# A cached-attention decode step: one load for the last two V tiles, and dummy matmuls on both sides of them

## The chip, the cores and the metric

The kernel runs on one core of a Trainium2 chip. The metric is the device time of one execution in microseconds (us). The kernel before takes 381.98 us, the median of three runs (381.79 to 382.12).

In what follows PE is the matmul engine (TensorE), DVE the vector engine, ACT the scalar engine, SP the engine whose queue issues the large loads. L464 is line 464 of the kernel.

## What is computed

One token (a row x of 1024) goes through two branches whose results are mixed by a gate. Branch A is attention with a cache of 65,536 positions: 32 query heads share 4 heads of K and V, each head 128 wide. Branch B is a small gated MLP.

```python
g = sigmoid((x * gate_w).sum(-1))
q = (x @ wq)                                   # 32 heads of 128
scores = einsum('bhqd,bhkd->bhqk', q, k) * 128 ** -0.5
p = softmax(scores)                            # over 65,536 positions
a = einsum('bhqk,bhkd->bhqd', p, v).reshape(1, 1, 4096) @ wo
b = branch_B(x)
out = g * a + (1 - g) * b                      # 1 x 1 x 1024, bf16
```

K and V are 4 x 65,536 x 128 in bf16 each, 67 MB each. With the weights some 162 MB are read for one row of output.

## The kernel before

One SBUF buffer `kv` has five places of 32 KB per partition. A K or V head is cut into four tiles (j = 0 to 3), each as large as one place, 4.2 MB. A load may span two places. All loads go through the one queue of SP, in program order; a load is issued when the last readers of its places are done.

```python
kv = big.tile([P, NKV * CT * P], BF16, name="kv")      # P = CT = 128, NKV = 5

def load_kv(src, g, j, at, n=1):                       # n tiles from tile j, into place `at`
    h, i = divmod(j, 2)
    rows = src[0, g, 2 * h * CT * P:2 * (h + 1) * CT * P, :].rearrange(
        "(p c) d -> p (c d)", c=2 * CT)
    v = load(rows[:, i * CT * DH:(i + n) * CT * DH], (n * CT * DH,), at)
    return [v[:, i * CT * DH:(i + 1) * CT * DH] for i in range(n)]
```

For every tile of V, 64 columns of probabilities are loaded as weights 16 times and two matmuls of 512 columns follow each load: 32 matmuls (L464). They go alternately to the upper and the lower half of the output's partitions and add up in one PSUM tile over all four tiles of the head.

```python
def v_tile(g, j, vt):
    ...
    for u in range(CC // 2):                           # CC = 32
        hs = slice(u % 2 * P // 2, (u % 2 + 1) * P // 2)
        for e in range(2):
            ins = nc.tensor.matmul(o_ps[g][hs, e, :], lhsT=ptt[g, j][:, 2 * u:2 * u + 2, :]...,
                                   rhs=vx[:, 2 * u + e], ...)          # L464
            if e > 0:
                same_weights(ins)                      # the second weight load is dropped
```

After the fourth tile `head_out` reduces this PSUM tile on DVE, sums over groups with two pairs of small matmuls on PE, divides by the softmax's sum and writes 32 rows of `oa`.

```python
def head_out(g):
    nc.vector.tensor_tensor(out=om8, in0=o_ps[g]..., in1=own_8..., op=ALU.mult)   # L474
    nc.vector.tensor_reduce(out=o_sb[:], in_=om8..., op=ALU.add)                  # L478
    nc.tensor.matmul(om_ps[gs, DH:], lhsT=hs, rhs=lss[g][:], ...)                 # L482
    nc.tensor.matmul(om_ps[gs, :DH], lhsT=hs, rhs=o_sb[:], ...)                   # L484
    ...                                                                           # five small DVE operations
    nc.vector.tensor_scalar(out=oa[gs, :], in0=osum[gs, :], ...)                  # L496

def keep_busy(n):                                      # dummy matmuls, their result is never read
    ps = pss.tile([P, 2 * HN], FP32, name="busy_ps", tag="s")
    for i in range(n):
        nc.tensor.matmul(ps[:, :HN], lhsT=w[:, :P], rhs=w[:, :HN], ...)           # L503, 128x128x512
```

The end of the kernel is the last head's V, its output, and then the projection with `wo`, which comes in five loads. Dummy matmuls stand where PE would have nothing to do. PE executes in program order.

```python
for j, n, at in ((0, 2, 2), (2, 1, 1), (3, 1, 0)):     # tiles 0 and 1, then 2, then 3
    for i, vt in enumerate(load_kv(A_v_cache, G - 1, j, at, n)):
        v_tile(G - 1, j + i, vt)
keep_busy(6)
head_out(G - 1)
keep_busy(16)

for n in (24, 4, 2, 1, 1):                             # of 32 pieces of wo, 256 KB each
    t = load(wo_view[:, c0:c0 + n, :], (n, D), 3 + c0 * D / (CT * P))   # places 3 and 4
    project(t, n, oa, c0, last=(c0 + n == OC))         # 4 n matmuls of 256 columns, L514
    keep_busy(WO_BUSY[n])                              # 24: 0, 4: 2, 2: 1, 1: 0
    c0 += n
nc.scalar.copy(out=out_sb[:], in_=out_ps[:])           # L566, then the store
```

Of the kernel before, what the change touches and what calls it, by code (L numbers as in the profile page):

```python
# [29 lines left out]
def kernel(  # L30
# [18 lines left out]
    _, G, S, DH = A_k_cache.shape  # L49
# [30 lines left out]
    def same_weights(ins):  # L80
        held.add(ins.ins.name)
# [95 lines left out]
    def load(src, shape, at):  # L177
        n = 1
        for s in shape:
            n *= s  # L180
        v = kv[:, int(at * CT * P):int(at * CT * P) + n]
        if len(shape) == 2:
            v = v.rearrange("p (a b) -> p a b", b=shape[1])
        ins = nc.sync.dma_start(out=v, in_=src)  # L184
        if not first_load:
            first_load.append(ins.ins.name)
        return v

    def load_kv(src, g, j, at, n=1):
# [5 lines that stand above are left out]
# [166 lines left out]
    for k in range(NHB):  # L361
# [3 lines left out]
                                                                   j=B, e=2),  # L365
# [91 lines left out]
    def v_tile(g, j, vt):  # L457
        if j == 0:
            o_ps[g] = pso.tile([P, 2, VC * DH], FP32, name="o_ps")
        vx = vt.rearrange("p (v c d) -> p c v d", v=VC, d=DH)  # L460
        for u in range(CC // 2):
            hs = slice(u % 2 * P // 2, (u % 2 + 1) * P // 2)
            for e in range(2):
                ins = nc.tensor.matmul(  # L464
                    o_ps[g][hs, e, :],
                    lhsT=ptt[g, j][:, 2 * u:2 * u + 2, :].rearrange("p c x -> p (c x)"),
                    rhs=vx[:, 2 * u + e], start=(j == 0 and u < 2),
                    stop=(j == NT - 1 and u >= CC // 2 - 2), skip_group_check=True)
                if e > 0:
                    same_weights(ins)  # L470

    def head_out(g):
        gs = slice(g * B, (g + 1) * B)
        nc.vector.tensor_tensor(  # L474
            out=om8, in0=o_ps[g][:].rearrange("p e (v d) -> p (e v) d", d=DH),
            in1=own_8[:].unsqueeze(2).to_broadcast([P, 2 * VC, DH]), op=ALU.mult)
        o_sb = wk.tile([P, DH], FP32, name="o_sb")
        nc.vector.tensor_reduce(out=o_sb[:], in_=om8.rearrange("p x d -> p d x"), axis=AX.X,  # L478
                                op=ALU.add)
        om_ps = psm.tile([P, DH + NT], FP32, name="om_ps", tag="m")  # L480
        hs = hsel[:].rearrange("p h q -> p (h q)")
        nc.tensor.matmul(om_ps[gs, DH:], lhsT=hs, rhs=lss[g][:], start=True, stop=True,  # L482
                         skip_group_check=True)
        nc.tensor.matmul(om_ps[gs, :DH], lhsT=hs, rhs=o_sb[:], start=True, stop=True,  # L484
                         skip_group_check=True)
        rl = wk.tile([P, 2], FP32, name="rl")
        nc.vector.reduce_sum(out=rl[gs, 0:1], in_=om_ps[gs, DH:], axis=AX.X)
        nc.vector.reciprocal(out=rl[gs, 1:2], in_=rl[gs, 0:1])
        om = wk.tile([P, QD, OC], FP32, name="om")
        nc.vector.tensor_tensor(  # L490
            out=om[gs], in0=om_ps[gs, :DH].rearrange("p (q c) -> p q c", c=OC),
            in1=own_q[gs, :].unsqueeze(2).to_broadcast([B, QD, OC]), op=ALU.mult)
        osum = wk.tile([P, OC], FP32, name="osum")
        nc.vector.tensor_reduce(out=osum[gs, :], in_=om[gs].rearrange("p q c -> p c q"),
                                axis=AX.X, op=ALU.add)
        nc.vector.tensor_scalar(out=oa[gs, :], in0=osum[gs, :], scalar1=rl[gs, 1:2],  # L496
                                scalar2=gate[gs, :], op0=ALU.mult, op1=ALU.mult)

    def keep_busy(n):
        ps = pss.tile([P, 2 * HN], FP32, name="busy_ps", tag="s")  # L500
        w = wt[G % 2][:].rearrange("p v b t u h -> p (v b t u h)")
        for i in range(n):
            ins = nc.tensor.matmul(ps[:, :HN], lhsT=w[:, :P], rhs=w[:, :HN], start=True,  # L503
                                   stop=True, skip_group_check=True)
            if i > 0:
                same_weights(ins)
# [22 lines left out]
    for g in range(1, G):  # L529
# [16 lines left out]
            if h == 0 and g + 1 < G:  # L546
                build_w(g + 1)
        head_out(g - 1)
    for j, n, at in ((0, 2, 2), (2, 1, 1), (3, 1, 0)):
        for i, vt in enumerate(load_kv(A_v_cache, G - 1, j, at, n)):  # L550
            v_tile(G - 1, j + i, vt)
    keep_busy(6)
    head_out(G - 1)
    keep_busy(16)

# [54 lines left out]
```

## Time and profile before

| | |
|---|---|
| time, median of three | 381.98 us |
| span of the profiled execution | 380.5 us |
| read from memory | 162.01 MB, 426 GB/s over the span |
| PE busy | 226.4 us, 60% |
| DVE busy | 211.2 us, 56% |
| ACT busy | 39.6 us, 10% |
| mean granted clock of PE | 0.839 of full speed |

The profile is that of one execution. A busy share is an average over the whole span. The row of slices cuts the span in 40 equal parts of 9.5 us; a digit is the busy share in tenths. The chain that ended last is followed back from the last instruction, at each step to what released it. The timeline lists the instructions of an engine in order of time, runs of the same kind merged; in brackets stands how long the engine was idle before and what ended that. A table by windows gives, for each stretch, its length, the busy time of PE, of its weight loads, of DVE, ACT and GpSimd (with the number of instructions), then the clock granted to PE (1.00 is full speed), the busy share of the DMA engines, and GB/s.

Matmuls are pipelined, so the time of a group is the distance from its first start to its last end, and the lengths of single matmuls in it overlap.

### The profile page before, as it was taken

The page shows a single profiled execution, that of the slowest core. Times are in us where ns is not written, and L with a number is a line of the kernel's source. Part 1 is how long each engine was busy: PE and PEld are TensorE (multiplying, and loading weights), DVE is VectorE, ACT ScalarE, POOL GpSimd, SP SyncE. Part 2 cuts the span into 40 slices and gives each one's busy share as a digit, 9 for nine tenths or more (in the row PEclk, how much of TensorE's full clock was granted, in tenths as well). Part 3 has the DMA queues.
Part 4 walks back from the last instruction along what each step waited for, and adds up shares of the span by engine and source line. Part 5 has one row for each costly group of instructions (what it writes and reads, how often), then busy time and mean ns, then how long its engine had stood idle before and what let it go on. Part 6 is the DMA issues. An engine that isn't in the chain of part 4 may idle for free.

```text
span 380.5 us, 2602 instructions
## 1 busy us (share of the span) xinstructions
PE 226.4 (60%) x1397; PEld 55.6 (15%) x800; DVE 211.2 (56%) x207; ACT 39.6 (10%) x55; POOL 4.4 (1%) x10
## 2 busy tenths in 40 slices
PE   0060605967655784794499139762993197739386
PEld 0010101211211210121022001110220011202113
DVE  4134217989374947867893058678940397650040
ACT  1001000111104310114011001140110010500000
POOL 4000000000000000000000000000000000000000
PEclk9995765999958796999599758995898599959789
DMA  9999999999999999999999999999999999999995
GB/s 386 476 420 413 401 442 441 441 472 410 407 422 441 441 443 434 434 434 441 441 429 441 434 441 420 422 413 442 434 434 429 427 434 442 436 410 434 431 432 224
DMA packets 3655, 162.17 MB, mean 426 GB/s; under 512 B 440, under 2 KB 444, under 8 KB 828
## 3 DMA queue, kind: packets, MB, share of 16 engines
q1 hardware_dynamic: 3604, 162.01, 98.8%
q8 instruction: 8, 0.13, 0.1%
q14 instruction: 3, 0.02, 0.0%
q10 hardware_dynamic: 40, 0.01, 0.0%
HBM read 162.01 MB, written 0.00 MB: 426 GB/s over the span
## 4 chain that ended last, share of the span: by engine, by line
DMA 71%; PE 17%; DVE 9%; issue 2%; SPq 0%; ACTq 0%; ACT 0%; DVEq 0%
DMA kv<-in_A_k_cache_dram 52%; PE s_ps L419 13%; DVE kv L412 8%; DMA kv<-in_A_wo_dram 7%; DMA kv<-in_A_v_cache_dram 7%; DMA wb<-in_B_b_sp_dram 5%; PE o_ps L464 2%; PE z_ps L296 1%; SPq L184 0%; DVE mx L402 0%; ACTq L198 0%; PE small_ps L271 0%; ACT out_sb L566 0%; PE out_ps L514 0%; ACTq L199 0%
## 5 line engine op out<-in xcount | busy, mean ns | idle before, releaser
L419 PE MATMUL s_ps<-kv,wt 128*128 128x512 bf16 x512 | 132.8, 414 | 81.4 <-DVE kv L412 81.3
L412 DVE STREAM_TRANSPOSE kv<-kv 128x2048 int32<-128x2048 int32 x64 | 142.4, 2280 | 69.7 <-DMA kv<-in_A_k_cache_dram 69.7
L464 PE MATMUL o_ps<-kv,pt 128*64 128x512 bf16 x512 | 63.6, 408 | 14.3 <-DMA kv<-in_A_v_cache_dram 14.3
L419 PEld LDWEIGHTS <-wt 128*128 128x128 bf16 x256 | 26.4, 103 | 189.2 <-issue 117.9
L428 ACT CAST sc<-s_ps 128x1024 bf16<-128x1024 f32 x16 | 16.2, 1013 | 250.7 <-PE s_ps L419 250.7
L464 PEld LDWEIGHTS <-pt 128*64 128x64 bf16 x256 | 16.9, 117 | 57.9 <-issue 48.6
L454 DVE STREAM_TRANSPOSE pt<-sc 128x1024 bf16<-128x1024 bf16 x16 | 18.6, 1217 | 6.8 <-ACT sc L451 6.8
L474 DVE TENSOR_TENSOR rowt<-o_ps,own 128x1024 f32<-128x1024 f32 x4 | 4.8, 1195 | 26.5 <-PE o_ps L464 26.5
L451 ACT ACTIVATE sc<-sc,nb 128x1024 bf16<-128x1024 bf16 x16 | 18.2, 1137 | 12.2 <-DVE nb L447 12.2
L484 PE MATMUL om_ps<-o_sb,hsel 128*32 128x128 f32 x8 | 2.3, 388 | 18.3 <-DVE o_sb L478 18.3
L402 DVE TENSOR_TENSOR mx<-mx,sc 128x1024 bf16<-128x1024 bf16 x8 | 5.5, 687 | 13.6 <-ACT sc L428 13.6
L296 PE MATMUL q_ps<-kv,xT 128*32 128x512 bf16 x64 | 5.7, 534 | 7.2 <-DMA kv<-in_A_wq_dram 7.2
L252 PE MATMUL xb_ps<-xg,spread 8*128 8x256 bf16 x1 | 0.4, 364 | 13.5 <-DMA xg<-in_gate_w_dram 13.5
L478 DVE TENSOR_REDUCE o_sb<-rowt 128x128 f32<-128x1024 f32 x4 | 7.5, 1872 | 0.1
L363 DVE TENSOR_TENSOR rowt<-q_ps,own_b 128x512 f32<-128x512 f32 x2 | 1.3, 686 | 10.8 <-PE q_ps L296 10.8
L503 PE MATMUL busy_ps<-wt 128*128 128x512 bf16 x25 | 6.1, 381 | 0.0
L296 PE MATMUL z_ps<-kv,xT 128*32 128x448 bf16 x64 | 6.1, 572 | 0.0
L566 ACT CAST out_sb<-out_ps 128x256 bf16<-128x256 f32 x1 | 0.4, 372 | 46.4 <-PE out_ps L514 46.4
L256 DVE TENSOR_TENSOR xm<-xb_ps,sel_i 128x128 f32<-128x128 f32 x2 | 0.5, 286 | 8.2 <-PE xb_ps L252 8.2
L514 PE MATMUL out_ps<-kv,oa 128*32 128x256 bf16 x128 | 4.2, 273 | 1.4 <-DMA kv<-in_A_wo_dram 1.4
L435 DVE TENSOR_REDUCE m<-mx 128x1 f32<-128x1024 bf16 x4 | 4.8, 1209 | 0.1
L296 PEld LDWEIGHTS <-xT 128*32 128x32 bf16 x64 | 2.6, 137 | 14.7 <-issue 14.6
(90 smaller groups left out, 61.2 us busy)
## 6 DMA issues: line engine op xcount, KB each, us to landing
kv<-in_A_v_cache_dram SPq DMA_DIRECT2D x2, 4096.0 KB, 22.8
kv<-in_B_w_in_dram SPq DMA_DIRECT2D x1, 7168.0 KB, 19.7
kv<-in_A_wo_dram SPq DMA_DIRECT2D x1, 6144.0 KB
kv<-in_B_w_out_dram SPq DMA_DIRECT2D x1, 3584.0 KB
kv<-in_A_wo_dram SPq DMA_DIRECT2D x1, 1024.0 KB, 26.8
kv<-in_A_wo_dram SPq DMA_DIRECT2D x1, 512.0 KB
kv<-in_A_wo_dram SPq DMA_DIRECT2D x2, 256.0 KB
kv<-in_A_k_cache_dram SPq DMA_DIRECT2D x8, 27.6
```

The costliest lines, as they stand in the source:

```text
L296: ins = nc.tensor.matmul(ps[t * B:(t + 1) * B, k * HN:k * HN + n], lhsT=xT[:, i * KH + c:i * KH + c + 1].to_broadcast([P, B]), rhs=w[:, c, ...
L402: nc.vector.tensor_tensor(out=mx[:], in0=mxs[g][:], in1=sc[:], op=ALU.max)
L412: nc.vector.transpose(out=kb[:, v * n:(v + 1) * n], in_=kb[:, v * n:(v + 1) * n])
L419: ins = nc.tensor.matmul(s_ps[:, k * HN:(k + 1) * HN], lhsT=wt[g % 2][:, v, b].rearrange("p a v h -> p (a v h)"), rhs=kx[:, b // 2, b % 2, ...
L428: nc.scalar.copy(out=sct[g, j][:], in_=s_ps[:])
L435: nc.vector.reduce_max(out=m1[:], in_=mxs[g][:], axis=AX.X)
L451: nc.scalar.activation(out=sct[g, j][:], in_=sct[g, j][:], func=ACT.Exp, scale=SCALE, bias=nb[:, 0:1], accum_out=lss[g][:, j:j + 1])
L454: nc.vector.transpose(out=ptt[g, j][:].rearrange("p c x -> p (c x)"), in_=sct[g, j][:])
L464: ins = nc.tensor.matmul(o_ps[g][hs, e, :], lhsT=ptt[g, j][:, 2 * u:2 * u + 2, :].rearrange("p c x -> p (c x)"), rhs=vx[:, 2 * u + e], sta ...
L474: nc.vector.tensor_tensor(out=om8, in0=o_ps[g][:].rearrange("p e (v d) -> p (e v) d", d=DH), in1=own_8[:].unsqueeze(2).to_broadcast([P, 2 ...
L478: nc.vector.tensor_reduce(out=o_sb[:], in_=om8.rearrange("p x d -> p d x"), axis=AX.X, op=ALU.add)
L503: ins = nc.tensor.matmul(ps[:, :HN], lhsT=w[:, :P], rhs=w[:, :HN], start=True, stop=True, skip_group_check=True)
```

## The change

Tiles 2 and 3 of the last head's V come in one load of 8.4 MB into places 0 and 1, where there were two loads of 4.2 MB. After tiles 0 and 1, PE gets 24 dummy matmuls; after tiles 2 and 3 it gets 6, as before. The 16 behind the head's output stay. The dummies are there to keep PE from idling while it waits for a load[...]. Nothing of the result changes.

```diff
-    for j, n, at in ((0, 2, 2), (2, 1, 1), (3, 1, 0)):
-        for i, vt in enumerate(load_kv(A_v_cache, G - 1, j, at, n)):
+    for j, at in ((0, 2), (2, 0)):
+        for i, vt in enumerate(load_kv(A_v_cache, G - 1, j, at, 2)):
             v_tile(G - 1, j + i, vt)
-    keep_busy(6)
+        keep_busy((24, 6)[j // 2])
     head_out(G - 1)
     keep_busy(16)
```

In the order of instructions PE gains the 24 dummies (and their one weight load) between tile 1 and tile 2, and tile 3 no longer has a wait for a load of its own. SP has one load less. The other engines' instructions are the same.

## The prediction

> **What bounds the kernel now.** I read the row of slices first. All 40 slices of the DMA row read 9 but the last, at 426 GB/s over the span, while PE is busy 60% and DVE 56%. So the stream of loads is the bound as a whole, and a change that moves no bytes can only act where the stream ends. Next the chain that ended last, by line, and the end of the same chain in order of time:
>
> ```profile
> DMA 71%; PE 17%; DVE 9%; issue 2%; SPq 0%; ACTq 0%; ACT 0%; DVEq 0%
> ...
> 350.46 27.89 DMA kv<-in_A_wo_dram
> 378.39 0.32 PE out_ps L514 x4
> 378.73 0.37 ACT out_sb L566
> ```
>
> The columns of the last three are start, length, what. The end hangs on the last piece of wo, landed near 378.35; behind it stand only four matmuls, one copy and the store. Then the timeline of PE over the last stage (start, length, engine, line, operation; in brackets the idle time before it and what ended it):
>
> ```profile
> 339.43 9.20 PE L464 MATMUL o_ps<-kv,pt 128*64 128x512 bf16 x64 [2.11 <-DMA kv<-in_A_v_cache_dram]
> 349.14 3.65 PE L464 MATMUL o_ps<-kv,pt 128*64 128x512 bf16 x32 [0.52 <-DMA kv<-in_A_v_cache_dram]
> 358.86 6.26 PE L464 MATMUL o_ps<-kv,pt 128*64 128x512 bf16 x32 [6.08 <-DMA kv<-in_A_v_cache_dram]
> 365.05 1.47 PE L503 MATMUL busy_ps<-wt 128*128 128x512 bf16 x6
> 366.45 0.23 PE L482 MATMUL om_ps<-ls,hsel 128*32 128x4 f32 x2
> 368.34 0.41 PE L484 MATMUL om_ps<-o_sb,hsel 128*32 128x128 f32 x2 [1.67 <-DVE o_sb L478]
> 368.68 3.63 PE L503 MATMUL busy_ps<-wt 128*128 128x512 bf16 x16
> 373.41 3.24 PE L514 MATMUL out_ps<-kv,oa 128*32 128x256 bf16 x112 [1.10 <-DMA kv<-in_A_wo_dram]
> ...
> 378.39 0.29 PE L514 MATMUL out_ps<-kv,oa 128*32 128x256 bf16 x4 [0.28 <-DMA kv<-in_A_wo_dram]
> ```
>
> To be seen: tile 2 of V is used up (349.14 to 352.79) while tile 3 is on its way; tile 3 lands at about 358.85. Before the projection PE waits 1.10 us for wo, before its last four matmuls 0.28 us. These 1.38 us are all the room that PE has behind tile 3.
>
> Last the granted clock (PEclk, third figure from the end; 1.00 full, 0.50 half) in windows cut where it changes:
>
> ```profile
> 118.44:121.85 3.41, 1.15 (x7) 0.37 (x3) 0.65 (x3) 2.28 (x2) 0.00 (x0) 1.00 1.20 519
> 350.54:353.96 3.42, 2.24 (x22) 0.68 (x9) 0.00 (x0) 0.00 (x0) 0.00 (x0) 1.00 0.91 393
> 353.96:357.37 3.41, 0.00 (x0) 0.00 (x0) 0.00 (x0) 0.00 (x0) 0.00 (x0) 1.00 1.07 461
> 357.37:360.78 3.41, 1.92 (x10) 0.58 (x5) 0.00 (x0) 0.00 (x0) 0.00 (x0) 0.50 1.07 461
> 360.78:364.20 3.42, 3.42 (x18) 0.91 (x8) 0.00 (x0) 0.00 (x0) 0.00 (x0) 0.50 1.03 446
> ```
>
> The first figure behind the length is PE's busy time. Stepping the whole trace in this way puts every change of the clock on one grid of 3.41 us. At full clock a window with 0.34 or less of PE busy (1.15 of 3.41 at 118.44) was followed by half clock, one with 0.42 or more (1.43 at 77.48) was not. At half clock 0.81 or more (2.77 at 125.27) brought it back, 0.72 or less (2.44 at 108.20) did not. I take the middles, 0.38 and 0.77.
>
> [...] two joined V or K loads land between 300.67 and 339.38, 19.36 us each; tiles 2 and 3 as two loads take from 339.38 to 358.82, 19.44 us.
>
> **The change part by part.**
>
> The load. One 8.4 MB load for two of 4.2 MB. Both were issued at 331.01, some 8 us ahead of their turn, and wo at 348.66, 10 us ahead of its own, on the matmuls of tile 1, which stand before the new dummies. The queue runs dry in neither form. Gain at the landing: 19.44 - 19.36 = 0.08 us, which I count as none. Tile 3 still lands near 358.85, but tile 2 now counts as landed only then too.
>
> The matmuls that move. The 32 matmuls of tile 2, 3.65 us hidden under tile 3's transfer before, now stand behind 358.85 with the other 32.
>
> The 24 dummies. At full clock 16 take 3.63 us (0.227 each), so 24 take 5.45 us: about 348.65 to 354.1. They leave PE idle for 358.85 - 354.1 = 4.75 us. Two neighbouring windows cannot share 4.75 us without one of them having 2.37 idle, busy share 0.30 or less. So the clock falls wherever the grid lies: the dummies are too few by about 1 us to hold it. What the grid decides is when it comes back.
>
> Time T of the 64 matmuls. Elsewhere in this trace 64 of the kind take 7.10 us at full clock (the group at 203.70). At half clock four take 0.85 us against 0.43, so a cold stretch c adds 0.495 c. (Check: tile 3, cold until 364.20, c = 5.34: 3.65 + 2.64 = 6.29, measured 6.26.) Let p be the time from the landing to the next edge of the grid. [...] I take p anywhere in 0 to 3.41:
> - p under 0.8: the clock is still up at the landing, falls at the edge, returns a window later; c = 3.41, T = 8.8.
> - p from 0.8 to 2.65: cold at the landing, that window too little busy; c = p + 3.41, T = 9.2 to 10.1, 9.6 on average.
> - p over 2.65: cold, back at the edge; c = p, T = 8.4 to 8.8.
>
> Weighted by 0.80, 1.85 and 0.76 of 3.41 the mean is 9.2 us.
>
> From there to the end. Before, tile 3 ends at 365.12 and the 16 dummies at 368.68 + 3.63 = 372.31, 7.19 us later. The projection with its dummies takes 4.99 us from its start if wo is there (373.41 to 378.68, less 0.28). So PE ends at 358.85 + T + 7.19 + 4.99 = 371.03 + T against 378.68: **the loss is T - 7.65**, nothing where that is negative. With 9.2 it is 1.55 us, from 0.8 to 2.5. In this the 16 dummies are the later wait: oa is ready 4.97 us after tile 3 (365.12 to 370.09), 373.0 with T = 9.2, the dummies end at 375.2. The first 6.3 MB of wo land at 373.41, the next 1.05 MB at 430 GB/s by 375.9, before PE has worked through the first.
>
> **Rivals.**
>
> *The clock holds.* If the bridge is good enough, T = 7.1, below 7.65: PE is ready before wo, nothing changes, 381.9. The aim of the change speaks for it; the 4.75 us gap against the 0.34 windows speaks against it. It would take dummies that run longer than 0.227 each or an earlier landing.
>
> *The load is hidden or a little faster.* The tail is DMA-bound, so a lower cost of the single load is the only thing that can shorten it: 0.08 us, 381.9. A saving several times that would need the boundary between two loads to cost time, and the DMA row shows no dip at 349. I give this little.
>
> *The dummies as the bound.* The 24 could delay tile 2 if they ran at half clock: 24 x 0.43 = 10.3 us, to 358.9, just at the landing. PE would count as busy all the time, and the clock would be up at the landing, T near 7.1. The first group's 9.20 us ends at full clock, so I set this aside.
>
> **Range and chances.** 381.98 + 1.55 = 383.5. The grid alone gives 382.8 to 384.5; a gap that starts or ends a little differently, or a clock that holds after all, reaches down to 382.2. I take 382.3 to 384.5. 2% is 7.6 us, three times the largest loss that I can construct: within 2% at 0.975, faster 0.01, slower 0.015.
>
> **What would show it.** Right: one group of 64 matmuls from about 358.9, lasting 8.4 to 10.1 us; the 24 dummies from about 348.65 to 354.1; a clock that reads 0.50 at some point between 356 and 365; no wait for wo left before the projection; the chain that ends last running through PE from the landing of V, with the DMA stream over 1 us or more before the last matmul. Wrong: a T near 7.1 at full clock throughout, the projection still waiting for wo, and a time within 0.3 us of before; or a landing of V or of wo that has moved by more than 0.3 us, which would mean that the load itself changed.

## The result and the profile after

The changed kernel takes 383.82 us (median of six runs, 383.77 to 384.54) against 381.84 us before (six runs). The ratio is 1.0055, 95% interval 1.0042 to 1.0068: slower by about 2 us, and within 2%.

The chain that ended last in the changed kernel, by engine, and its last pieces in order of time (start, length, what):

```profile
DMA 56%; PE 22%; DVE 16%; issue 4%; ACT 1%; ACTq 0%; DVEq 0%
```

```profile
331.35 27.73 DMA kv<-in_A_v_cache_dram
359.07 0.04 issue
359.12 10.05 PE o_ps L464 x64
...
370.45 1.88 DVE o_sb L478
...
372.78 3.56 PE busy_ps L503 x16
376.34 3.17 PE out_ps L514 x112
...
381.08 0.37 ACT out_sb L566
```

Loads have 56% of the chain where they had 71%. The 27.89 us of wo, 7% of the span, are no longer in it; the rest of the difference lies ahead of 300 us, where nothing was changed. From the landing of V at 359.07 to the end everything is PE and DVE, and 3.56 us of it are dummies. The timeline of PE over the same stretch, to be laid beside the one of before:

```profile
339.74 9.49 PE L464 MATMUL o_ps<-kv,pt 128*64 128x512 bf16 x64 [2.10 <-DMA kv<-in_A_v_cache_dram]
349.16 5.35 PE L503 MATMUL busy_ps<-wt 128*128 128x512 bf16 x23
359.12 10.04 PE L464 MATMUL o_ps<-kv,pt 128*64 128x512 bf16 x64 [4.60 <-DMA kv<-in_A_v_cache_dram]
...
372.71 3.63 PE L503 MATMUL busy_ps<-wt 128*128 128x512 bf16 x16
376.27 3.24 PE L514 MATMUL out_ps<-kv,oa 128*32 128x256 bf16 x112
...
380.63 0.40 PE L514 MATMUL out_ps<-kv,oa 128*32 128x256 bf16 x8
```

The trace shows 23 of the 24 dummies; a record is missing. The wait of 1.10 us ahead of the projection and that of 0.28 us ahead of its end are gone: no bracket stands behind either line. The last matmul ends at 381.03 instead of 378.68, 2.35 us later, and this execution took 384.24 us against 381.88 for the profiled one of before, 2.36 us more. Nothing else is needed to account for it.

The clock, in windows of 3.41 us cut where it changes (the first figure behind the length is PE's busy time, the third from the end the granted clock):

```profile
351.44:354.86 3.42, 3.08 (x15) 0.11 (x1) 0.00 (x0) 0.00 (x0) 0.00 (x0) 1.00 0.80 345
354.86:358.27 3.41, 0.00 (x0) 0.00 (x0) 0.00 (x0) 0.00 (x0) 0.00 (x0) 1.00 1.09 471
358.27:361.68 3.41, 2.56 (x13) 0.82 (x7) 0.00 (x0) 0.00 (x0) 0.00 (x0) 0.50 1.03 447
361.68:365.10 3.42, 3.42 (x20) 0.93 (x8) 0.00 (x0) 0.00 (x0) 0.00 (x0) 0.50 0.86 374
```

The 24 dummies kept one window more busy (3.08 of 3.42 us) and left the next one empty (0.00). The clock fell at 358.27, at the end of the empty one and 0.85 us before the data came, and stayed down until 365.10.

### The profile page after: what moved, and what is told of

The parts are those of the page before. It is cut to its first block, busy times and chain, and to the rows that moved or that the text cites. A ratio compares the mean times of both kernels' runs of the same rounds, so it can differ in the third digit from the quotient of the medians.

```text
span 382.8 us, 2622 instructions
## 1 busy us (share of the span) xinstructions
PE 231.3 (60%) x1418; PEld 55.4 (14%) x801; DVE 211.2 (55%) x207; ACT 39.6 (10%) x55; POOL 4.4 (1%) x10
## 4 chain that ended last, share of the span: by engine, by line
DMA 56%; PE 22%; DVE 16%; issue 4%; ACT 1%; ACTq 0%; DVEq 0%
DMA kv<-in_A_k_cache_dram 45%; PE s_ps L419 13%; DVE kv L412 12%; DMA kv<-in_A_v_cache_dram 7%; PE o_ps L464 5%; DMA wb<-in_B_b_sp_dram 5%; DVE pt L454 1%; PE busy_ps L503 1%; PE out_ps L514 1%; DVE o_sb L478 1%; PE z_ps L296 1%; DVE mx L402 1%; DVE rowt L474 1%; ACT sc L428 1%; ACT sc L451 0%
## 5 line engine op out<-in xcount | busy, mean ns | idle before, releaser
L464 PE MATMUL o_ps<-kv,pt 128*64 128x512 bf16 x512 | 64.4, 413 | 13.7 <-DMA kv<-in_A_v_cache_dram 13.7
L503 PE MATMUL busy_ps<-wt 128*128 128x512 bf16 x46 | 11.1, 380 | 0.1
L296 PE MATMUL z_ps<-kv,xT 128*32 128x448 bf16 x64 | 4.8, 476 | 0.0
```

What stands on the lines that cost most here:

```text
L296: ins = nc.tensor.matmul(ps[t * B:(t + 1) * B, k * HN:k * HN + n], lhsT=xT[:, i * KH + c:i * KH + c + 1].to_broadcast([P, B]), rhs=w[:, c, ...
```

## The experiments

Theory A is the one of the prediction: 64 matmuls now stand behind the landing, part of them at half clock, and the dummies and the projection follow in program order. Rival B: the joined load itself costs time. Rival C: the 24 dummies cost time by themselves. Times are medians, with the range of single runs; a ratio is to the kernel before, run in the same group.

### Joined load, no dummies behind tile 1

```diff
-        keep_busy((24, 6)[j // 2])
+        if j == 2:
+            keep_busy(6)
```

> The joined load without the 24 dummies behind tile 1 (0 and 6). Theory A (64 matmuls behind the landing, part of them at half clock; the end moves by T - 7.65 us): PE idles some 10 us before the landing instead of 4.6, the clock is down in both, so T stays 8.4 to 10.1 us and the time 382.7 to 384.4 us, within 0.5 of the changed kernel's 383.8. Rival B (the joined load itself costs time): 383.8 as well. Rival C (the 24 dummies cost the time): back at 381.9.

Measured: 382.96 us (382.18 to 383.37), ratio 1.003 (1.002 to 1.004). PE idled 9.42 us and the 64 matmuls took 8.80:

```profile
358.74 8.80 PE L464 MATMUL o_ps<-kv,pt 128*64 128x512 bf16 x64 [9.42 <-DMA kv<-in_A_v_cache_dram]
```

So the 24 dummies gain nothing where they stand; without them it is still slower than before the change, which speaks against C as the whole cause. But the median is 0.9 us under that of the changed kernel, more than the 0.5 that A allowed.

### The changed kernel once more

No edit. It was run to see whether those 0.9 us belong to the dummies.

> The changed kernel itself once more, to stand beside the runs of this group: the joined kernel without the 24 dummies came out 0.9 us lower than the changed one had on another occasion, where theory A expected no difference. Theory A (the grid of the clock decides, and lies differently from execution to execution): 382.7 to 384.5 us, single times spread, T of the profiled one between 8.4 and 10.1. Rival C (the 24 dummies cost something by themselves): 383.8 again, single times close together.

Measured: 383.45 us (382.40 to 384.15), ratio 1.0042 (1.0030 to 1.0054). The times are spread as A has it. In the profiled execution the clock fell at 358.46, was back at 361.88, and the 64 matmuls took 8.69 us:

```profile
358.62 8.69 PE L464 MATMUL o_ps<-kv,pt 128*64 128x512 bf16 x64 [4.25 <-DMA kv<-in_A_v_cache_dram]
```

The same program thus takes 8.69 or 10.04 us here, with the clock back 3.26 or 5.98 us after V landed. The interval overlaps that of the kernel without the 24 dummies. The spans of the core say more. A time holds some 1.4 us outside the span in most runs, but 2.2 to 2.6 in a few, two of these six among them. By the spans alone the changed kernel has a median of 382.4 us the first time and 381.4 the second, the kernel without the 24 dummies 381.5, the kernel before 380.3 to 380.4. One and the same program thus differs between two occasions by 1.0 us, so the 0.9 us are no sign that the 24 dummies cost time by themselves. A cost of a few tenths is not ruled out here.

### More dummies: 36, then 44

```diff
-        keep_busy((24, 6)[j // 2])
+        keep_busy((36, 6)[j // 2])
```

> The joined load with 36 dummies behind tile 1 instead of 24. Theory A: 36 x 0.2275 = 8.2 us leave a gap of 1.8 us before the landing near 359; no window of 3.41 us is then less than 0.47 busy, the clock holds, T = 7.1 us, under 7.65: 381.9 us as before the change, and the projection waits for wo again. Rival B (the joined load itself): 383.8, as it is still joined. Rival C (the dummies cost): 383.8 or more, as there are 12 more.

Measured: 382.08 us (381.61 to 383.78, 21 runs), ratio 1.0012 (1.0005 to 1.0019). The expectation came true in part: by the span of the core, 14 of the 21 runs lie at 380.0 to 380.5 us, the level of before, and seven at 380.7 to 381.2. The profiled execution, at 382.47, shows why in its timeline of PE and in two windows of the clock:

```profile
347.69 7.94 PE L503 MATMUL busy_ps<-wt 128*128 128x512 bf16 x35
358.58 8.79 PE L464 MATMUL o_ps<-kv,pt 128*64 128x512 bf16 x64 [2.94 <-DMA kv<-in_A_v_cache_dram]
```

```profile
355.82:359.23 3.41, 0.65 (x7) 0.25 (x4) 0.00 (x0) 0.00 (x0) 0.00 (x0) 1.00 0.80 346
359.23:362.64 3.41, 3.41 (x19) 0.95 (x9) 0.00 (x0) 0.00 (x0) 0.00 (x0) 0.50 1.07 461
```

Tile 1 was done at 347.69 here, not at 349.1, because the clock had come up earlier in tiles 0 and 1 (at 342.17, against 344.62 in the changed kernel's first profile). So the 36 dummies ended at 355.6 and left 2.94 us. The clock was still up when the data came (358.58) and fell 0.65 us later (359.23), at the end of a window with 0.65 us of PE busy. A bridge of fixed length has to cover the earliest end of what stands before it (347.69 here), so 44 were tried:

> The joined load with 44 dummies behind tile 1. With 36 the gap was 2.9 us in the profiled execution, as tile 1 was done 1.5 us earlier than I had taken, and the clock fell. Theory A: 44 x 0.2275 = 10.0 us end between 357.6 and 359.2, the gap is at most 1.2 us, no window can lose the clock, T = 7.1 us at full clock in every execution, the projection waits for wo, 381.8 us, single times within 0.4 us of one another. Rival B (the joined load costs): above 382.5. Rival C (dummies cost): 383 or more.

Measured: 381.80 us (381.68 to 382.26), ratio 1.0000 (0.9992 to 1.0008).

```profile
348.82 9.67 PE L503 MATMUL busy_ps<-wt 128*128 128x512 bf16 x44
358.84 7.10 PE L464 MATMUL o_ps<-kv,pt 128*64 128x512 bf16 x64 [0.34 <-DMA kv<-in_A_v_cache_dram]
...
373.40 3.24 PE L514 MATMUL out_ps<-kv,oa 128*32 128x256 bf16 x112 [0.27 <-DMA kv<-in_A_wo_dram]
...
378.41 0.29 PE L514 MATMUL out_ps<-kv,oa 128*32 128x256 bf16 x4 [0.32 <-DMA kv<-in_A_wo_dram]
```

The 64 matmuls take 7.10 us, the waits for wo are back, and the time is that of before. The load is joined (it lands at 358.84, the last one of before at 358.86) and there are 20 dummies more than in the changed kernel, and neither costs more than the 0.3 us of the interval: B falls, and C falls as the cause of the loss.

### Joined load, 6 dummies instead of 16 behind the head's output

```diff
     head_out(G - 1)
-    keep_busy(16)
+    keep_busy(6)
```

> The changed kernel with 6 dummies instead of 16 behind the last head's output. Theory A: T stays 8.4 to 10.1 us, but the projection starts about 4.97 us after the last V matmul (when oa is there) instead of 7.19: the loss becomes T - 9.9, that is none up to 0.2 us, 381.9 to 382.2 us. Rival B: 383.8, a later or slower load is not touched. Rival C (the 24 dummies): 383.8.

Measured: 381.72 us (381.62 to 382.18), ratio 0.9999 (0.9991 to 1.0007). The 64 matmuls are as slow as ever, but the projection no longer stands behind 16 dummies:

```profile
358.60 9.37 PE L464 MATMUL o_ps<-kv,pt 128*64 128x512 bf16 x64 [5.25 <-DMA kv<-in_A_v_cache_dram]
...
371.53 1.47 PE L503 MATMUL busy_ps<-wt 128*128 128x512 bf16 x6
373.16 3.24 PE L514 MATMUL out_ps<-kv,oa 128*32 128x256 bf16 x112 [0.15 <-DMA kv<-in_A_wo_dram]
```

So the whole loss passed through those dummies. In the kernel before they fill a wait for wo that the change has closed.

### Two loads as before, with the 24 dummies behind tile 1

```diff
             v_tile(G - 1, j + i, vt)
+        if j == 0:
+            keep_busy(24)
```

> The kernel before, its two loads kept apart, with the 24 dummies added behind tile 1. Theory A: the dummies delay tile 2 to about 354 to 358, so PE is at full clock when tile 3 lands near 358.9; its 32 matmuls take 3.7 us instead of 6.3, the projection waits some 3.5 us or more for wo instead of 1.1, and the time is 381.9 us, as the loads set the end. Rival B (joining costs): 381.9. Rival C (the dummies cost): 383.8.

Measured: 382.85 us (381.85 to 384.39), ratio 1.0035 (1.0022 to 1.0049). A miss: A had expected no change. Tile 3 did run at full clock, and that was the trouble, as timeline and windows show:

```profile
358.62 3.65 PE L464 MATMUL o_ps<-kv,pt 128*64 128x512 bf16 x32 [1.03 <-DMA kv<-in_A_v_cache_dram]
...
365.82 3.63 PE L503 MATMUL busy_ps<-wt 128*128 128x512 bf16 x16
373.15 5.73 PE L514 MATMUL out_ps<-kv,oa 128*32 128x256 bf16 x112 [3.70 <-DMA kv<-in_A_wo_dram]
```

```profile
368.06:371.47 3.41, 1.39 (x7) 0.09 (x1) 0.00 (x0) 0.00 (x0) 0.00 (x0) 1.00 0.94 396
371.47:374.88 3.41, 1.73 (x36) 1.45 (x39) 0.00 (x0) 0.00 (x0) 0.00 (x0) 0.50 0.87 358
```

PE was ready earlier, ran out of dummies at 369.45, idled 3.70 us until wo came, and lost the clock at 371.47. The projection took 5.73 us instead of 3.24, with nothing behind it to hide the difference. If that is the cause, more dummies in this second gap must undo it (16 to 32 behind the head's output, all else the same):

> The kernel before with 24 dummies behind tile 1, and 32 instead of 16 behind the head's output. With 16 the head's output came 2.9 us earlier, PE then idled 3.7 us before wo landed, the clock fell and the projection ran at half clock (5.73 us for 112 matmuls instead of 3.24). Theory A: 32 x 0.2275 = 7.3 us from about 365.8 end at 373.1, the gap to wo is gone, the projection takes 3.2 us, 381.8 us. Rival C (the 24 dummies cost by themselves): it stays at 382.8 or above.

Measured: 381.95 us (381.59 to 382.96), ratio 1.0004 (0.9996 to 1.0012). The wait for wo is 0.26 us, the projection takes 3.24:

```profile
365.92 7.08 PE L503 MATMUL busy_ps<-wt 128*128 128x512 bf16 x32
373.25 3.24 PE L514 MATMUL out_ps<-kv,oa 128*32 128x256 bf16 x112 [0.26 <-DMA kv<-in_A_wo_dram]
```

### The kernel before, with 30 dummies instead of 16

```diff
     head_out(G - 1)
-    keep_busy(16)
+    keep_busy(30)
```

> The kernel before with 30 dummies instead of 16 behind the head's output: 14 x 0.2275 = 3.2 us more on PE, nothing joined, no dummies behind tile 1. Theory A (PE's work in program order behind the landing of tile 3 sets the end once it uses up the 1.4 us of room): tile 3 takes 5.0 to 6.6 us by where the grid lies, the end moves by 0.5 to 2.2 us, 382.3 to 384.0 us, and PE no longer waits for wo. Rival (the dummies lie beside the stream of loads and are hidden): 381.8.

Measured: 382.64 us (381.79 to 383.44), ratio 1.0018 (1.0010 to 1.0025). The 14 dummies added 3.02 us to PE (6.65 us for 30, against 3.63 for 16), and 0.8 us of it reached the median:

```profile
358.63 5.27 PE L464 MATMUL o_ps<-kv,pt 128*64 128x512 bf16 x32 [6.07 <-DMA kv<-in_A_v_cache_dram]
...
367.46 6.65 PE L503 MATMUL busy_ps<-wt 128*128 128x512 bf16 x30
374.04 3.24 PE L514 MATMUL out_ps<-kv,oa 128*32 128x256 bf16 x112
```

Tile 3 took 5.27 us in this execution where it took 6.26 in the profile of before, as the clock was back after 3.3 us (at 361.96) instead of 5.3 (at 364.20). That enlarges the room for dummies from 1.38 to 2.37 us, and in this execution, at 382.01 us, the last matmul ends at 378.80, only 0.12 us later than before. The order of PE's work behind the last landing is thus a bound of its own once the room is used up, without any joined load.

None of these versions is faster than the kernel before. The three without a loss (44 dummies; 6 behind the output; 24 and 32 with two loads) come to the same 381.7 to 382.0 us, as their profiled executions all end on the last piece of wo.

## Why the prediction was right

It said 383.5 us, 382.3 to 384.5; measured were 383.82 and, the second time, 383.45. By its steps:

- *The landing does not move.* Predicted near 358.85; 359.12 after, 358.84 with 44 dummies; over all the traces here 358.58 to 359.12 with the joined load, 358.62 to 358.86 with two. The joined load brought nothing that could be measured (ratio 1.0000 with the clock held).
- *The dummies are too few.* Predicted from about 348.65 to 354.1 with a gap of 4.75 us; measured 349.16 to 354.51 and 4.60 us. The clock fell in both profiled executions of the changed kernel, at 358.27 and 358.46.
- *T = 7.1 + 0.495 c.* This term held best. With c, the cold time among the 64 matmuls, read off the clock's changes:

| kernel | full clock from | c, us | T by the formula | T measured |
|---|---|---|---|---|
| 44 dummies | (never lost) | 0 | 7.10 | 7.10 |
| changed, second time | 361.88 | 3.26 | 8.71 | 8.69 |
| 36 dummies | 362.65 | 3.42 | 8.79 | 8.79 |
| no dummies behind tile 1 | 362.23 | 3.49 | 8.83 | 8.80 |
| 6 behind the output | 363.24 | 4.64 | 9.40 | 9.37 |
| changed, first time | 365.10 | 5.98 | 10.06 | 10.04 |

Each of the three cases by p, the time from the landing to the next edge of the grid, was met: p = 0.65 with 36 dummies, where the clock fell at the edge and c was 3.42; p = 2.57 in the first profile of the changed kernel, with c = p + 3.41; p = 3.26 in the second, with c = p.

- *The loss is T - 7.65.* Right in kind, but a little too large. The stretch from the projection to the end was put at 4.99 us and is 4.76 when wo is there (376.27 to 381.03), since its last two groups of four run as one. With that the loss is T - 7.9. For the profiled execution, 10.04 - 7.9 is 2.1, and 0.27 from the later landing makes 2.4, against 2.36 measured.
- *The 16 dummies are the later wait.* Shown by taking ten of them away: the loss was gone.
- *The average over the grid* gave 1.55 us. That p is anywhere in 0 to 3.41, each value as likely as another, was the author's estimate; the five traces with the joined load in which the clock fell have p = 0.08, 0.65, 1.22, 2.57 and 3.26. The medians are 2.0 and 1.6 us above before, the spans 2.0 and 1.0 us. With T - 7.9 in place of T - 7.65 the same average would have been 1.3 us. That 383.5 lies so near the medians is thus in part luck: the single spans of the changed kernel run from 381.0 to 382.8 us, and six runs each do not tell whether the grid really falls evenly.

The rivals of the prediction: the clock that holds was not seen with 24 dummies; with 44 it gave 381.80 us and 64 matmuls of 7.10 us, where 381.9 and 7.1 had been said. The load that is a little faster stayed invisible. Dummies that run at half clock were not seen: 23 recorded ones took 5.35 us, 35 took 7.94 and 44 took 9.67. What the prediction had not thought of is the gap on the other side: that a faster tile 3 would by itself lengthen the wait for wo (3.70 us with two loads and 24 dummies, against 1.10), and that the clock would fall in this wait too (at 371.47).

## What to carry to other kernels

Here splitting the last load paid not by its bytes but by what the engine could do with the first half while the second was on its way (32 matmuls, 3.65 us); before joining loads at the end of a stream, count the work that moves behind the landing, at the clock that the wait will leave (0.50 here, after 4.60 us). The dummies of this kernel were as long as the gap was on the day they were sized. Moving the work ahead of them turned them into a delay (the 16 behind the head's output: 383.82 us, and 381.72 with 6) or left the next piece cold (the projection: 5.73 us instead of 3.24), so size the gaps on both sides anew together. A bridge must cover the earliest end of the work before it (347.69 with 36 dummies), not the usual one (349.16 in the first profile of the changed kernel).

## What was not expected of the hardware

- The changes of the clock lie on a grid of 3.41 us in every trace here. Nine of the traces (all but that of 44 dummies) were stepped from end to end in windows of 3.41 us, and each of the 209 changes lies at an edge of these windows. In the kernel before, four of the changes are at 333.48, 343.72, 357.37 and 364.20: 10.24, 13.65 and 6.83 us apart, that is 3, 4 and 2 windows. With 44 dummies the two changes seen in steps of 0.5 us lie near 333.97 and 344.21, 10.24 us apart. The edges lie differently in each trace: the last one before 360 is at 357.37 in the kernel before, at 358.27 and 358.46 in the two of the changed kernel, at 359.82 with 6 dummies behind the output.
- No single busy time divides the windows that were followed by half clock from those that were not, and some above the 0.38 of a window that the prediction took from a single trace were followed by it. In the nine traces, from the first record of the clock on (at 23 to 27 us), all 99 windows of 3.41 us at full clock with up to 1.31 us of PE busy (0.38; 6 dummies behind the output, at 209.64) were followed by half clock. Between 1.36 and 1.61 us both occur: 27 windows were followed by full clock, as with 1.39 us (no dummies behind tile 1, at 314.44), and six by half clock, as with 1.39 us (two loads with 24 dummies, at 368.06) and 1.61 us (0.47; 6 behind the output, at 117.48). Since some records of matmuls are missing (one of the 24 dummies above) and their ends are modelled, the traces do not say it more closely. In the profile with 36 dummies a wait of 2.94 us, 2.76 of it ahead of an edge in one window, was followed by half clock.
- The way back up agrees with the 0.77 of the prediction in all nine traces: windows at half clock with up to 2.59 us of PE busy (0.76; two loads with 24 dummies, at 224.70) were followed by half clock again, those with 2.66 us (0.78; 30 dummies, at 146.92) or more by full clock. The window shown above at 358.27, with 2.56 us, is of the first kind: the first profile of the changed kernel was back at 365.10. In the second the window at 358.46 had 3.25 us, and the clock was back at 361.88, one window after its start.
- The clock can fall after the work has begun again: with 36 dummies it did so 0.65 us into the matmuls, at the end of the window in which most of the wait lay.
